# First MoE as x w2 w_out plus the positive part of two differences, its weights in memory by half tiles

## The chip, the cores and the metric

One core of one Trainium2 chip runs the whole program in one launch. The metric is the device time of one execution in microseconds. The kernel before took 809.39 us, the median of three runs from 806.94 to 810.66.

## What is computed

The reference has three stages on 4 x 768 = 3072 tokens of 384 values:

```python
for t in range(S):                                   # attention: B 4, H 8, S 768, D 48
    new_re = ar * S_re - ai * S_im                   # ar, ai: a_re, a_im, normalised
    new_im = ar * S_im + ai * S_re
    S_re, S_im = (new_re + kv, new_im)               # kv: outer product of k and v at t
    y[:, :, t] = np.einsum('bhd,bhde->bhe', q[:, :, t], S_re)

h = np.maximum(np.maximum(x @ w1, x @ w2), x @ w3)   # first MoE: 384 -> 768
x = h @ w_out                                        # 768 -> 384

for e in range(E):                                   # second MoE: 8 experts, one for each token
    mask = expert_idx == e
    h = np.maximum(x[mask] @ w1[e], 0.0)
    out[mask] = gate_w[mask, None] * (h @ w2[e])
```

The expert of a token is the largest of eight scaled cosines with `expert_emb`. Weights of the first MoE and `w_out` arrive as float64.

## The kernel before

**Two phases.** `phase1` does attention and the first MoE, `phase2` the second. Phase one takes the tokens in NU = 12 units of 256, three a batch. For unit u, `front(u)` normalises a, `mid(u)` builds prefix products of a on DVE (`sa`, `sb`, `Ct`, `X`), `back(u)` multiplies q and k by them and by their inverse (`m`, `rr`, `QK`) and DMAs the result into the matmul operand S (`S<-QK`). `attn(u, ch)` takes a tile of 128 tokens: products `pk`, `pa`, masked on DVE to `at`; `pT` and the running state; `py`; and y as x in two parts, `xhi` (ACT, rounded to f32r) and `xlo` (the rest, DVE or ACT). The 24 tiles are numbered 0 to 23, so `py20` is `py` of tile 20. `moe1(u)` is the first MoE. `route_early` sorts the first TE = 22 tiles' tokens to experts near the end of phase one. Phase two gathers the tokens by expert and runs the second MoE (lines 1268 to 1334).

**The first MoE, `moe1` (line 818).** Products of f32 precision are made of three f32r ones: hi by hi, hi by lo, lo by hi. For each of three groups `f2` of 256 of the 768 columns, and for each of w1, w2, w3 (m), two tiles of 128 columns take nine products of 256 tokens each, into PSUM tile `ph` (ring `h`, 3 buffers). ACT copies the first `ph` to `h`, DVE takes the maximum with the second and the third. For two of the groups (SPLIT = 2) ACT rounds `h` to `hhi` (1 buffer), DVE subtracts it into `hlo` (it shares the 2 buffers of `h`), and `px` gets three products of 392 columns for each f; the third group multiplies `h` itself in f32 by `wo`. The 392 columns are 384 of `w_out` and 8 of `w_out` times the normalised `expert_emb`, which give the routing logits.

**Weights, `weights` (line 709).** 24 tiles of 128 x 384 float64 words, six of `w_out` and eighteen halves of w1, w2, w3, are loaded as pairs of 32-bit words by POOL's DMA queue, and made into f32 from their bits: a sign (one of SIGNS = 4 tiles on DVE, the others by two ACT instructions), a scaled copy on ACT, two `scalar_tensor_tensor` on DVE. ACT then rounds the tile to its high part, and PE subtracts that from it in PSUM and ACT copies the rest:

```python
s.copy(hi, f)
t.matmul(pd, self.ident, f, start=True, stop=False)
t.matmul(pd, self.minus, hi, start=False, stop=True)
s.copy(rest, pd)
```

`ident` is f32 and `minus` the negated identity in f32r. The six tiles of `w_out` come first, then the others by m, i and half. There are 22 of these pairs, since the last two tiles of `w_out` stay f32. Raw tiles of w1 to w3 land in the memory of parts that are not yet written.

**Order.** `phase1` is not issued as written. `Recorder` (line 124) records each instruction with a key (KEYS: conv -0.9, attn -2.0, moe 0.3 and so on, plus the unit) and a bias for each kind and engine (BIAS, line 372), plans an order with modelled costs, and issues each engine's instructions in that order (line 368 in every row below). `keep_warm` (line 620, rows of L627) puts products that nobody reads into PE's gaps. Each engine works through its own order; SP's and POOL's are the DMA queues.

Of the kernel before, what the change touches and what calls it, by code (L numbers as in the profile page):

```python
# [9 lines left out]
F32 = mybir.dt.float32  # L10
# [11 lines left out]
W = 256  # L22
# [3 lines left out]
DM = H * D  # L26
# [97 lines left out]
class Recorder:  # L124
# [203 lines left out]
    def issue(self):  # L328
# [30 lines left out]
        for i in seq:  # L359
# [12 lines left out]
    BIAS = {"Gs": 1.84, "QKrg": -1.81, "Sg": 1.17, "Ss": 0.07, "Tss": 0.78, "Xv": 0.43, "arenv": 0.65, "cvhv": 0.53,  # L372
            "embss": -0.15, "fms": 2.46, "fmv": 3.34, "fyv": 0.76, "h_s": 0.7, "h_v": -0.65, "kt_s": -0.33, "pa_t": 1.07,
            "ph__t": -0.59, "pk_t": 1.3, "px__t": 0.15, "rrs": -0.38, "rrv": -0.75, "rwhig": -0.62, "rwlog": 1.88,
            "sav": -0.63, "slott": 2.08, "whi_s": 0.47, "wlo_s": 1.99, "xhis": 1.21, "xss": 0.26}
# [7 lines left out]
class Prog:  # L383
# [325 lines left out]
    def weights(self, split=True):  # L709
# [32 lines left out]
        ring, first = 0, 2 * self.SPLIT if split else 0  # L742
        for k, (src, m, i, c) in enumerate(todo):

            spot = None
            if split and m is not None:
                j = spots.index((m, i)) + (c > 0)
# [23 lines left out]
            whole = m is None and i >= first  # L771
            o = self.wo[:, i - first, :DM] if whole else f if split else self.w[:, m, i, c:c + n]
            v.scalar_tensor_tensor(o.bitcast(I32), raw[:, :, 0], 29, h, op0=ALU.logical_shift_right, op1=ALU.bitwise_or)
            if split and not whole:
                if m is not None and c == 0:
                    j = spots.index((m, i))
                    self.whi[m, i], self.wlo[m, i] = [self.tl(self.mw, [128, FF], f"w{x}{j}", 1, f"w{x}_{m}{i}", F32R)
                                                      for x in ("hi", "lo")]
                hi, rest = (self.wohi[:, i, :DM], self.wolo[:, i, :DM]) if m is None else \
                    (self.whi[m, i][:, c:c + n], self.wlo[m, i][:, c:c + n])  # L780
# [17 lines left out]
            if m is None and i == 5:  # L798
                if first:
                    s.copy(self.wohi[:, :, DM:], pG[:, :first])  # L800
                    v.tensor_sub(self.wolo[:, :, DM:], pG[:, :first], self.wohi[:, :, DM:].bitcast(F32))
                if first < 6:
                    v.tensor_copy(self.wo[:, :, DM:], pG[:, first:])
# [14 lines left out]
    def moe1(self, u):  # L818
# [5 lines left out]
        def mm(o, m, f):  # L824
            c = slice(f * 128, (f + 1) * 128)
            with q.group():
                for n, (w, x, i) in enumerate((w, x, i) for w, x in ((self.whi, xhi), (self.wlo, xhi), (self.whi, xlo))
                                              for i in range(3)):
                    t.matmul(o, w[m, i][:, c], x[:, i], start=n == 0, stop=n == 8)
        px = [self.tl(self.pf, [128, XC], "x1", 2, f"px1_{u}_{i}") for i in range(2)]  # L830
        for f2 in range(3):
            ps = []
            for m in range(3):
                ps.append(self.tl(self.pf, [128, 2, W], "h", 3, f"ph{u}_{f2}_{m}"))
                for f in range(2):
                    mm(ps[m][:, f], m, 2 * f2 + f)
# [5 lines left out]
            if f2 >= self.SPLIT:  # L842
                q.key = key
                for tt in range(2):
                    with q.group():
                        for f in range(2):
                            t.matmul(px[tt], h[:, f, tt * 128:tt * 128 + 128], self.wo[:, 2 * (f2 - self.SPLIT) + f],
                                     start=f2 + f == 0, stop=f2 + f == 3)
                continue
            hi = self.tl(pm, [128, 2, W], "hhi", 1, f"hhi{u}_{f2}", F32R)  # L850
            s.copy(hi, h)
            lo = self.tl(pm, [128, 2, W], "h", 2, f"hlo{u}_{f2}", F32R)
            v.tensor_sub(lo, h, hi.bitcast(F32))
# [196 lines left out]
    def phase1(self):  # L1050
        nc, tc = self.nc, self.tc
        with ExitStack() as ctx:
# [9 lines left out]
            self.wo = mw.tile([128, 6 - 2 * self.SPLIT, XC], F32, name="wo")  # L1062
            self.wohi = mw.tile([128, 2 * self.SPLIT, XC], F32R, name="wohi")
# [698 lines left out]
```

## Time and profile before

| | |
|---|---|
| Runs | 806.94, 809.39, 810.66 us |
| Profiled execution, its time | 811.25 us |
| Its span | 809.4 us, 19242 instructions |
| Mean granted clock of TensorE | 0.977 |
| PE, PEld | 750.9 us, 93%; 690.7 us, 85% |
| DVE, ACT, POOL | 78%, 55%, 12% |
| DMA | 107.46 MB, mean 133 GB/s |
| Weights converted, then the first `ph` | at 98.54 us |
| End of the last `px` of phase one, first product of the second MoE | 543.0 and 545.38 us |

The span is the time from the first to the last event of the profiled execution, whose own time is 1.9 us longer. A row of a group gives line, engine, operation, output<-inputs, shapes and count, then busy time, the mean length of one in ns, and idle time before them with what ended it. A row of a timeline gives its start and its busy time in us; xN stands for N like instructions in a row. Matmuls overlap, so what one costs is the distance between the starts of two. An f32 product is recorded as two matmuls. PE is the matrix engine, PEld its weight loads, PEclk the clock granted to it as a share of the full one, 1.2 of 2.4 GHz being 0.5.

### The profile page before, as it was taken

The page shows a single profiled execution, that of the slowest core. Times are in us where ns is not written, and L with a number is a line of the kernel's source. Part 1 is how long each engine was busy: PE and PEld are TensorE (multiplying, and loading weights), DVE is VectorE, ACT ScalarE, POOL GpSimd, SP SyncE. Part 2 cuts the span into 40 slices and gives each one's busy share as a digit, 9 for nine tenths or more (in the row PEclk, how much of TensorE's full clock was granted, in tenths as well). Part 3 has the DMA queues.
Part 4 walks back from the last instruction along what each step waited for, and adds up shares of the span by engine and source line. Part 5 has one row for each costly group of instructions (what it writes and reads, how often), then busy time and mean ns, then how long its engine had stood idle before and what let it go on. Part 6 is the DMA issues. An engine that isn't in the chain of part 4 may idle for free. (4 is left out here: it accounts for less than half of the span.)

```text
span 809.4 us, 19242 instructions
## 1 busy us (share of the span) xinstructions
PE 750.9 (93%) x7705; PEld 690.7 (85%) x7705; DVE 630.2 (78%) x1244; ACT 445.2 (55%) x1018; POOL 100.5 (12%) x156
## 2 busy tenths in 40 slices
PE   1757899999999999999999999999999999999996
PEld 0635789989898989999898989889989898989885
DVE  8999999999999999999988822659996455555420
ACT  8998746646647465665355341228545456554521
POOL 6301000000000000000000000021113312223111
PEclk9778999999999999999999999999999999999998
DMA  9706262571717345261624060051029694782500
GB/s 360 286 1 157 38 157 65 137 184 32 186 52 150 93 108 135 66 143 59 151 70 102 14 110 2 21 216 41 28 81 420 217 387 145 255 341 74 179 21 25
DMA packets 28754, 107.46 MB, mean 133 GB/s; under 512 B 5060, under 2 KB 8179, under 8 KB 25568
## 3 DMA queue, kind: packets, MB, share of 16 engines
q1 hardware_dynamic: 20432, 77.55, 32.2%
q0 software_dynamic: 7952, 28.21, 10.6%
q8 instruction: 62, 1.02, 0.5%
q10 hardware_dynamic: 272, 0.39, 0.2%
q14 instruction: 36, 0.29, 0.1%
HBM read 96.35 MB, written 10.62 MB: 132 GB/s over the span
## 5 line engine op out<-in xcount | busy, mean ns | idle before, releaser
L368 PE MATMUL ph<-xhi,whi 128*128 128x256 f32 x648 | 118.4, 291 | 0.4 <-DVE h L368 0.4
L368 PE MATMUL ph<-xlo,whi 128*128 128x256 f32 x648 | 113.0, 283 | 0.6 <-DVE xlo L368 0.6
L368 PE MATMUL ph<-xhi,wlo 128*128 128x256 f32 x648 | 112.7, 283 | 0.0
L368 PEld LDWEIGHTS ph<-xhi,whi 128*128 128x128 f32 x648 | 93.3, 191 | 6.9 <-issue 3.5
L368 PEld LDWEIGHTS ph<-xlo,whi 128*128 128x128 f32 x648 | 93.1, 192 | 1.0 <-DVE xlo L368 1.0
L368 PEld LDWEIGHTS ph<-xhi,wlo 128*128 128x128 f32 x648 | 93.0, 191 | 0.0
L1312 PE MATMUL ph<-xh,w1s 128*128 128x256 f32 x264 | 77.7, 294 | 0.0
L1274 DVE TENSOR_TENSOR w2l<-queue_q_buf,w2h 128x768 fp32r<-128x768 f32 x52 | 47.9, 955 | 37.3 <-ACT w2h L1273 37.3
L1312 PE MATMUL ph<-xh,w1l 128*128 128x256 f32 x264 | 75.4, 286 | 0.0
L1312 PE MATMUL ph<-xl,w1s 128*128 128x256 f32 x264 | 75.3, 285 | 0.0
L1328 PE MATMUL py<-w2h,hlo 128*128 128x384 f32 x200 | 67.1, 336 | 3.0 <-DVE hlo L1317 3.0
L1328 PE MATMUL py<-w2h,hhi 128*128 128x384 f32 x200 | 68.5, 343 | 0.0
L1328 PE MATMUL py<-w2l,hhi 128*128 128x384 f32 x200 | 67.1, 335 | 0.0
L368 DVE TENSOR_TENSOR h<-ph,h 128x512 f32<-128x512 f32 x72 | 49.5, 688 | 16.4 <-PE ph L368 15.0
L368 POOL DMA_DIRECT2D v<-v x24 | 13.0, 540 | 391.5 <-PE py L368 389.6
L1317 DVE SCALAR_TENSOR_TENSOR hlo<-ph,hhi 128x512 fp32r<-128x512 f32 x50 | 34.3, 687 | 32.7 <-ACT hhi L1316 32.6
L1316 ACT ACTIVATE hhi<-ph 128x512 fp32r<-128x512 f32 x50 | 29.9, 598 | 48.5 <-PE ph L1312 48.3
L1312 PEld LDWEIGHTS ph<-xh,w1s 128*128 128x128 f32 x264 | 51.2, 194 | 3.8 <-issue 3.1
L1312 PEld LDWEIGHTS ph<-xh,w1l 128*128 128x128 f32 x264 | 51.2, 194 | 0.5
L1312 PEld LDWEIGHTS ph<-xl,w1s 128*128 128x128 f32 x264 | 51.2, 194 | 0.0
L368 PE MATMUL pa<-S 112*128 112x128 f32 x384 | 49.1, 277 | 1.3 <-DVE at L368 0.7
L1273 ACT CAST w2h<-queue_q_buf 128x768 fp32r x52 | 40.7, 832 | 16.6 <-PE py L1328 15.5
(401 smaller groups left out, 1818.2 us busy)
## 6 DMA issues: line engine op xcount, KB each, us to landing
queue_q_buf<-w SPq DMA_DIRECT2D x26, 1536.0 KB
S<-QK SPq DMA_DIRECT2D x46, 289.1 KB
X<-a SPq DMA_DIRECT2D x11, 768.0 KB
QKr<-qk SPq DMA_DIRECT2D x11, 768.0 KB
w1m<-w SPq DMA_DIRECT2D x5, 1536.0 KB
w2m<-w SPq DMA_DIRECT2D x5, 1536.0 KB
v<-v POOLq DMA_DIRECT2D x24, 224.0 KB, 4.4
x1d<-x1s SPq DMA_DIRECT2D x22, 192.0 KB
```

The source lines that it names most:

```text
L368: getattr(getattr(self.nc, c[0]), c[1])(*c[2], **c[3])
L1273: s.copy(hi, b[:, c])
L1274: v.tensor_sub(lo, bv[:, c], hi.bitcast(F32))
L1312: t.matmul(ph[:, f], a, b, start=o == 0, stop=o == len(ops) - 1)
L1316: s.activation(hi, ph, AF.Relu).ins,
L1317: v.scalar_tensor_tensor(lo, ph, 0.0, hi.bitcast(F32), op0=ALU.max, op1=ALU.subtract).ins]
L1328: t.matmul(py, a[:, f, r], c[:, k % 4], start=o == 0, stop=o == 3 * KF - 1)
```

## The change

It rests on max(a, b, c) = b + max(0, a - b, c - b), so that the first MoE is x (w2 w_out) + max(0, x (w1 - w2), x (w3 - w2)) w_out.

- The host passes w2 a second time, transposed (`w2t`, six tiles of float64); tiles of w2 itself are no longer loaded. Tiles loaded are 24 again: six of `w2t` first (into the third buffer of ring `X`), then the first halves of w1 and w3, then the second halves, then `w_out`.
- For each half tile of w1 and w3 PE puts the f32 tile into PSUM and takes three transposed blocks of w2 off it by f32 products with `minus`; ACT rounds the difference to hi, PE subtracts that, ACT copies lo (`rest`). Both parts lie in the memory of the raw half tile.
- V = w2 w_out (384 x 392) is made by 18 f32 products (`pw0` to `pw2`, six each) and split into `vhi`, `vlo`.
- In `moe1`, V adds 18 f32r products of 392 columns to `px` at the start of a unit (at the end of it for unit 0). Two `ph` tiles for each group are left of three; ACT's copy becomes a Relu; one DVE maximum is left of two.
- `w_out` is split into `wohi`, `wolo` at the end, by four ACT copies and four DVE subtractions.
- BIAS, the table of biases, has other numbers. Lines after the table shift by up to 25.

```diff
@@ in the class Recorder
-    BIAS = {"Gs": 1.84, "QKrg": -1.81, "Sg": 1.17, "Ss": 0.07, "Tss": 0.78, "Xv": 0.43, "arenv": 0.65, "cvhv": 0.53,
...
+    BIAS = {"Cts": -0.91, "Cv": 0.78, "Gs": -0.3, "QKrv": -1.34, "QKs": -0.19, "Sg": 1.22, "Ss": 0.13, "Xg": 1.31,
...
@@ in weights
-        spots = [(m, i) for i in range(3) for m in range(3)]
-        todo = [(self.io["wo"][i], None, i, None) for i in range(6)]
-        todo += [(self.io["w123"][m, i, :, c:c + n], m, i, c) for m, i in spots for c in (0, n)]
+        out = [(self.io["wo"][i], None, i, None) for i in range(6)]
+        if split:
+            spots = [(m, i) for i in range(3) for m in (0, 2)]
+            todo = [(self.io["w2t"][f], 1, f, None) for f in range(6)]
+            w2t = self.tl(self.pp, [128, 3, L, 3 * NR], "X", 3, "w2t").rearrange("p c l b -> p (c l b)")
...
+        todo += [(self.io["w123"][m, i, :, c:c + n], m, i, c) for c in (0, n) for m, i in spots]
+        todo = todo + out
...
+        def rest(hi, lo, ps):
+            s.copy(hi, ps)
+            t.matmul(ps, self.minus, hi, start=False, stop=True, skip_group_check=True)
+            s.copy(lo, ps)
...
-                spot = f"w{'hi' if c else 'lo'}{j}" if j < len(spots) else None
-            if spot:
-                raw = self.tl(self.mw, [128, FF], spot, 1, "r" + spot, I32)
+            if split and c is not None:
+                raw = self.tl(self.mw, [128, FF], f"w{m}{i}{c}", 1, f"r{m}{i}{c}", I32)
...
-                    self.whi[m, i], self.wlo[m, i] = [self.tl(self.mw, [128, FF], f"w{x}{j}", 1, f"w{x}_{m}{i}", F32R)
...
-                s.copy(hi, f)
+                both = self.tl(self.mw, [128, 2, n], f"w{m}{i}{c}", 1, f"w_{m}{i}{c}", F32R)
+                self.whi[m, i, c // n], self.wlo[m, i, c // n] = both[:, 0], both[:, 1]
                 pd = self.tl(self.pf, [128, n], "h", 3, f"pd{k}")
                 with q.group():
-                    t.matmul(pd, self.ident, f, start=True, stop=False)
-                    t.matmul(pd, self.minus, hi, start=False, stop=True)
-                s.copy(rest, pd)
+                    t.matmul(pd, self.ident, f, start=True, stop=True)
+                    for b in range(3):
+                        t.matmul(pd[:, b * 128:(b + 1) * 128], w2t[:, c // 128 + b, i * 128:(i + 1) * 128],
+                                 self.minus.bitcast(F32), start=False, stop=True, skip_group_check=True)
+                rest(both[:, 0], both[:, 1], pd)
...
+        for f in range(2 * self.SPLIT):
+            s.copy(self.wohi[:, f], self.wo[:, f])
+            v.tensor_sub(self.wolo[:, f], self.wo[:, f], self.wohi[:, f].bitcast(F32))
+        for i in range(3):
+            pw = self.tl(self.pf, [128, XC], "h", 3, f"pw{i}")
+            with q.group():
+                for f in range(6):
+                    t.matmul(pw, w2t[:, f, i * 128:(i + 1) * 128], self.wo[:, f], start=f == 0, stop=f == 5)
+            rest(self.vhi[:, i], self.vlo[:, i], pw)
@@ in moe1
+        late = u == 0
+
+        def by_v():
+
+            for tt in range(2):
+                ts = slice(tt * 128, tt * 128 + 128)
+                with q.group():
+                    for n, (x, w, i) in enumerate((x, w, i) for x, w in ((xhi, self.vhi), (xhi, self.vlo), (xlo, self.vhi))
+                                                  for i in range(3)):
+                        t.matmul(px[tt], x[:, i, ts], w[:, i], start=n == 0 and not late, stop=n == 8 and late)
+        if not late:
+            by_v()
...
-            for m in range(3):
+            for m in (0, 2):
...
-            s.copy(h, ps[0])
+            s.activation(h, ps[0], AF.Relu)
             v.tensor_max(h, ps[1], h)
-            v.tensor_max(h, ps[2], h)
...
+        if late:
+            by_v()
@@ in the host's preparation of the inputs
+    w2t = f(i["moe_w2"][perm].T).reshape(6, 128, DM).view(np.int64)
```

The BIAS table and the new order of tiles move instructions on all engines. The places where the prediction speaks of that follow; numbers after names tell buffers apart.

DVE ahead of `xlo0`, the last operand of the first unit of the first MoE, before:

```order
L368 TENSOR_TENSOR sb_392<-Ct_144,X2_261 128x48
L368 TENSOR_TENSOR QKr1_260<-QKr1_260,rr1_329 128x768
L368 TENSOR_TENSOR Ct_144<-sb_392 128x24
L368 SCALAR_TENSOR_TENSOR xlo0_274<-py1_284,xhi0_273 128x3x128
L368 TENSOR_TENSOR sb_393<-Ct_144,X2_261 128x48
L368 SCALAR_TENSOR_TENSOR fm3_380<-fy3_381,X3_334 128x768
L368 TENSOR_TENSOR Ct_144<-sb_393 128x24
L368 SCALAR_TENSOR_TENSOR rr1_329<-rr1_329,QKr1_260 128x768
L368 TENSOR_TENSOR sb_394<-Ct_144,X2_261 128x48
L368 TENSOR_TENSOR QK1_330<-QKr1_260,X1_173 128x6x256
L368 TENSOR_TENSOR Ct_144<-sb_394 128x24
L368 TENSOR_TENSOR QK1_330<-rr1_329,X1_173 128x6x128
```

And now:

```order
L368 TENSOR_TENSOR rr1_311<-rr1_311 128x768
L368 TENSOR_TENSOR at1_1_268<-pa1_1_267,mask_66 128x512
L368 SCALAR_TENSOR_TENSOR rr1_311<-rr1_311,QKr1_245 128x768
L368 TENSOR_TENSOR X2_246<-sa_367 128x2x96
L368 SCALAR_TENSOR_TENSOR X2_246<-sa_367 128x96
L368 SCALAR_TENSOR_TENSOR fm3_359<-fy3_360,X3_316 128x768
L368 TENSOR_TENSOR sb_370<-X2_246 128x48
L368 TENSOR_TENSOR QK1_312<-rr1_311,X1_166 128x6x128
L368 TENSOR_TENSOR Ct_146<-sb_370 128x24
L368 TENSOR_TENSOR QK1_312<-rr1_311,X1_166 128x6x128
L368 TENSOR_TENSOR sb_371<-Ct_146,X2_246 128x48
L368 SCALAR_TENSOR_TENSOR xlo0_259<-py1_269,xhi0_258 128x3x128
```

The last `rr1` row, the three `QK1` rows (the widest of them, 128x6x256, ten rows above the piece) and the first `fm3` row stand ahead of `xlo0` now; they stood behind it.

PE in the attention of unit 0 (`pk0`, `pa0`, then `pT0`), before:

```order
L368 MATMUL pk0_1_265<-ident_61,S0_142 128x112 x4
L368 MATMUL pa0_1_269<-S0_142 128x128 x4
L368 MATMUL pd18_221<-cvh0_154,ident_61 128x384
L368 MATMUL pd18_221<-whi_02_219,minus_138 128x384
L368 MATMUL pk0_0_263<-ident_61,S0_142 128x112 x4
L368 MATMUL pd19_223<-cvh1_155,ident_61 128x384
L368 MATMUL pd19_223<-whi_02_219,minus_138 128x384
L368 MATMUL pa0_0_267<-S0_142 128x128 x4
L368 MATMUL pk1_0_276<-ident_61,S0_142 128x112 x4
L368 MATMUL pd20_227<-S1_143,ident_61 128x384
L368 MATMUL pd20_227<-whi_12_225,minus_138 128x384
```

And now:

```order
L368 MATMUL pk0_1_250<-ident_61,S0_144 128x112 x4
L368 MATMUL pG_204<-enT_164,wt22_214 128x8
L368 MATMUL pG_204<-enT_164,wt23_216 128x8 x3
L368 MATMUL pa0_1_254<-S0_144 128x128 x4
L368 MATMUL pw0_217<-wo_135,w2t_158 128x392 x6
L368 MATMUL pk0_0_248<-ident_61,S0_144 128x112 x4
L368 MATMUL pw1_218<-wo_135,w2t_158 128x392 x6
L368 MATMUL pa0_0_252<-S0_144 128x128 x4
L368 MATMUL pk1_0_261<-ident_61,S0_144 128x112 x4
L368 MATMUL pw2_219<-wo_135,w2t_158 128x392 x6
```

Where pairs `pd18` to `pd20` stood between the pieces of the attention, the three parts of the fold w2 w_out stand now.

DVE ahead of the `at` of tile 20 (`h9`: the first MoE of unit 9, `m11`: `back(11)`), before:

```order
L368 TENSOR_TENSOR h9_0_923<-ph9_0_1_921,h9_0_923 128x512
L368 TENSOR_TENSOR m11_0_1030<-X11_891,C11_1016 128x768
L368 TENSOR_TENSOR h9_0_923<-ph9_0_2_922,h9_0_923 128x512
L368 TENSOR_TENSOR m11_0_1030<-X11_891,C11_1016 128x768
L368 TENSOR_TENSOR hlo9_0_925<-h9_0_923,hhi9_0_924 128x512
L368 TENSOR_TENSOR X11_891<-m11_0_1030 128x2x384
L368 TENSOR_TENSOR m11_1_1031<-X11_891,C11_1016 128x768 x2
L368 TENSOR_TENSOR h9_1_929<-ph9_1_1_927,h9_1_929 128x512
L368 TENSOR_TENSOR X11_891<-m11_1_1031 128x2x384
L368 TENSOR_TENSOR h9_1_929<-ph9_1_2_928,h9_1_929 128x512
L368 TENSOR_TENSOR QK11_1029<-QKr11_963,X11_891 128x6x256
L368 TENSOR_TENSOR at20_0_970<-pa20_0_969,mask_66 128x512
```

And now:

```order
L368 TENSOR_TENSOR hlo9_0_882<-h9_0_880,hhi9_0_881 128x512
L368 TENSOR_TENSOR m11_0_982<-X11_849,C11_968 128x768 x2
L368 TENSOR_TENSOR X11_849<-m11_0_982 128x2x384
L368 TENSOR_TENSOR m11_1_983<-X11_849,C11_968 128x768 x2
L368 TENSOR_TENSOR X11_849<-m11_1_983 128x2x384
L368 TENSOR_TENSOR h9_1_885<-ph9_1_2_884,h9_1_885 128x512
L368 TENSOR_TENSOR QK11_981<-QKr11_918,X11_849 128x6x256
L368 TENSOR_TENSOR arena_1019<-mask_66,ident_61 128x128
L368 MEMSET arena_1019 128x176
L368 SCALAR_TENSOR_TENSOR rr11_980<-rr11_980 128x768
L368 MEMSET arena_1019 128x8
L368 TENSOR_TENSOR at20_0_925<-pa20_0_924,mask_66 128x512
```

Of the maxima of a group (`h9_1<-ph9_1_1`, `h9_1<-ph9_1_2`) one is left, and an `rr11` row stands ahead of `at20_0`.

## Rows read from the trace of the kernel before

**Rows 1.** The page, part 1: busy us (share of the span) xinstructions.

```profile
PE 750.9 (93%) x7705; PEld 690.7 (85%) x7705; DVE 630.2 (78%) x1244; ACT 445.2 (55%) x1018; POOL 100.5 (12%) x156
```

**Rows 2.** Stretches of the span; columns PE, PEld, DVE, ACT, POOL, PEclk, DMA, GB/s.

```profile
60.00:80.00 20.00, 14.85 (x71) 11.12 (x71) 19.97 (x51) 16.97 (x39) 2.74 (x5) 0.84 0.61 158
120.00:160.00 40.00, 39.31 (x516) 36.19 (x515) 38.76 (x75) 26.60 (x75) 1.10 (x2) 1.00 0.39 103
360.00:400.00 40.00, 40.00 (x445) 36.24 (x444) 38.59 (x86) 19.99 (x59) 1.07 (x2) 1.00 0.46 109
460.00:500.00 40.00, 40.00 (x427) 37.38 (x420) 12.56 (x18) 12.52 (x40) 1.07 (x2) 1.00 0.33 62
545.00:809.00 264.00, 251.23 (x1873) 236.32 (x1873) 153.66 (x264) 133.31 (x201) 60.53 (x56) 0.98 0.45 171
```

**Rows 3.** DVE's waits, 120 to 440 us: total, times, longest.

```profile
DVE fy L368 <- ACT fm L368: 3.0, 3, 1.8
```

**Rows 4.** PE's waits, 120 to 440 us.

```profile
PE pk L368 <- DMA S<-QK: 3.2, 4, 1.2
```

**Rows 5.** PE's timeline at the first `ph`: start, busy, instruction.

```profile
98.54 0.52 PE L368 MATMUL ph<-xhi,whi 128*128 128x256 f32 x3
```

**Rows 6.** PE's timeline: `pd` of the setup, `px` and `ph` of a unit.

```profile
71.16 0.81 PE L368 MATMUL pd<-S,ident 128*128 128x384 f32 x2
...
71.97 0.70 PE L627 MATMUL pk<-ident 128*128 128x112 f32 x5
...
79.92 1.64 PE L368 MATMUL pd<-cvh,ident 128*128 128x384 f32 x2 [1.69 <-ACT wlo L368]
...
81.68 0.63 PE L368 MATMUL pa<-S 112*128 112x128 f32 x2
...
472.68 0.34 PE L368 MATMUL px<-wolo,hhi 128*128 128x392 f32 x1
472.86 0.34 PE L368 MATMUL px<-wohi,hlo 128*128 128x392 f32 x1
...
479.00 0.52 PE L368 MATMUL ph<-xhi,wlo 128*128 128x256 f32 x3
479.36 0.52 PE L368 MATMUL ph<-xlo,whi 128*128 128x256 f32 x3
```

**Rows 7.** PE's timeline, `py20` and the last `px` of phase one.

```profile
459.46 1.05 PE L368 MATMUL py<-at,v 128*32 128x128 f32 x32
...
540.36 2.79 PE L368 MATMUL px<-wo,h 128*128 128x392 f32 x8
...
545.38 0.83 PE L1312 MATMUL ph<-xT,w1s 128*128 128x128 f32 x6
```

**Rows 8.** DVE's timeline at `xlo0` and between 445 and 464 us.

```profile
98.84 0.56 DVE L368 SCALAR_TENSOR_TENSOR xlo<-py,xhi 128x384 fp32r<-128x384 f32 x1
...
445.02 0.69 DVE L368 TENSOR_TENSOR h<-ph,h 128x512 f32<-128x512 f32 x1
445.62 0.95 DVE L368 TENSOR_TENSOR m<-X,C 128x768 f32<-128x768 f32 x1
446.49 0.68 DVE L368 TENSOR_TENSOR h<-ph,h 128x512 f32<-128x512 f32 x1
...
453.64 1.75 DVE L368 TENSOR_TENSOR QK<-QKr,X 128x1536 f32<-128x1536 f32 x1
455.31 1.28 DVE L368 TENSOR_TENSOR at<-pa,mask 128x512 f32<-128x512 f32 x2
...
462.19 1.83 DVE L368 TENSOR_TENSOR QK<-rr,X 128x768 f32<-128x768 f32 x2
```

**Rows 9.** Groups of DVE and ACT by line, 120 to 440 us.

```profile
L368 DVE TENSOR_TENSOR h<-ph,h 128x512 f32<-128x512 f32 x50 | 34.4, 687 | 1.3 <-PE ph L368 0.8
...
L368 ACT COPY h<-ph 128x512 f32<-128x512 f32 x25 | 14.6, 585 | 18.9 <-DVE hlo L368 15.3 <-PE ph L368 3.6
...
L368 ACT CAST hhi<-h 128x512 fp32r<-128x512 f32 x17 | 10.5, 619 | 20.9 <-PE px L368 12.1 <-DVE h L368 8.5
```

More of the change, by code (lines that the diff above doesn't have):

```diff
@@ L741, in weights @@
         v.tensor_copy(enT, ps)
-        ring, first = 0, 2 * self.SPLIT if split else 0
-        for k, (src, m, i, c) in enumerate(todo):
-            spot = None
-            if split and m is not None:
-                j = spots.index((m, i)) + (c > 0)
-                spot = f"w{'hi' if c else 'lo'}{j}" if j < len(spots) else None
-            if spot:
-                raw = self.tl(self.mw, [128, FF], spot, 1, "r" + spot, I32)
+        ring = 0
+        def rest(hi, lo, ps):
+            s.copy(hi, ps)
+            t.matmul(ps, self.minus, hi, start=False, stop=True, skip_group_check=True)
+            s.copy(lo, ps)
+        for k, (src, m, i, c) in enumerate(todo):
+            if split and c is not None:
+                raw = self.tl(self.mw, [128, FF], f"w{m}{i}{c}", 1, f"r{m}{i}{c}", I32)
             else:
@@ L798, in weights @@
             if m is None and i == 5:
[L799 to L803, printed above, removed]
+                v.tensor_copy(self.wo[:, :, DM:], pG)
+        if not split:
+            return
+        for f in range(2 * self.SPLIT):
[7 more added lines that the diff above has]
+            rest(self.vhi[:, i], self.vlo[:, i], pw)
     def sqrt_small(self, new, out, x, n):
@@ L824, in mm @@
         def mm(o, m, f):
-            c = slice(f * 128, (f + 1) * 128)
+            half, c = f // 3, slice(f % 3 * 128, f % 3 * 128 + 128)
             with q.group():
@@ L828, in mm @@
                                               for i in range(3)):
-                    t.matmul(o, w[m, i][:, c], x[:, i], start=n == 0, stop=n == 8)
+                    t.matmul(o, w[m, i, half][:, c], x[:, i], start=n == 0, stop=n == 8)
         px = [self.tl(self.pf, [128, XC], "x1", 2, f"px1_{u}_{i}") for i in range(2)]
+        late = u == 0
[8 more added lines that the diff above has]
+            by_v()
         for f2 in range(3):
             ps = []
-            for m in range(3):
+            for m in (0, 2):
                 ps.append(self.tl(self.pf, [128, 2, W], "h", 3, f"ph{u}_{f2}_{m}"))
                 for f in range(2):
-                    mm(ps[m][:, f], m, 2 * f2 + f)
+                    mm(ps[-1][:, f], m, 2 * f2 + f)
             h = self.tl(pm, [128, 2, W], "h", 2, f"h{u}_{f2}")
             key, q.key = q.key, u + self.KEYS["max"]
-            s.copy(h, ps[0])
+            s.activation(h, ps[0], AF.Relu)
             v.tensor_max(h, ps[1], h)
-            v.tensor_max(h, ps[2], h)
[L842 to L853, printed above, removed]
+            if f2 < self.SPLIT:
+                hi = self.tl(pm, [128, 2, W], "hhi", 1, f"hhi{u}_{f2}", F32R)
+                s.copy(hi, h)
+                lo = self.tl(pm, [128, 2, W], "h", 2, f"hlo{u}_{f2}", F32R)
+                v.tensor_sub(lo, h, hi.bitcast(F32))
             q.key = key
@@ L858, in moe1 @@
                         ts = slice(tt * 128, tt * 128 + 128)
-                        wh, wl = self.wohi[:, 2 * f2 + f], self.wolo[:, 2 * f2 + f]
-                        for k, (a, b) in enumerate(((hi, wh), (hi, wl), (lo, wh))):
-                            t.matmul(px[tt], a[:, f, ts], b, start=f2 + f + k == 0, stop=f2 + f + k == 5)
+                        if f2 < self.SPLIT:
+                            wh, wl = self.wohi[:, 2 * f2 + f], self.wolo[:, 2 * f2 + f]
+                            terms = (hi, wh), (hi, wl), (lo, wh)
+                        else:
+                            terms = (h, self.wo[:, 2 * f2 + f]),
+                        for k, (a, b) in enumerate(terms):
+                            t.matmul(px[tt], a[:, f, ts], b, start=late and f2 + f + k == 0,
+                                     stop=not late and f2 + f == 3 and k == len(terms) - 1)
+        if late:
+            by_v()
         for tt in range(2):
```

29 lines of the change are left out of this document (14 added, 15 removed).

## Prediction, made before the changed kernel was run

> **What bounds the kernel now.** I read the page's busy times first, then a table of stretches, then the waits of the two busy engines, then single rows. The page gives TensorE (PE) 93% of the span, its weight loads (PEld) 85%, VectorE (DVE) 78% and ScalarE (ACT) 55% [rows 1]; these are averages over three stages. The stretches tell them apart [rows 2]. From 120 to 400 us, where twelve units of 256 tokens go through attention and the first MoE, PE is busy 39.3 to 40.0 of 40 us and DVE 38.6 to 38.8. At 460 to 500 us DVE has only 12.6 of 40 to do and PE 40.0: the tail is PE's alone. From 545 us on the second MoE runs, 264 us with PE busy 251; the change does not enter it, so it only shifts. Before 100 us weights are converted, PE is busy 14.9 of 20 us at a granted clock of 0.84, and DVE is busy 19.97 of 20.
>
> Two engines can be busy while one waits for the other in small pieces. From 120 to 440 us DVE's longest sum of waits is 3.0 us, for an `fm` of ACT [rows 3], and PE's is 3.2 us, for a DMA [rows 4]. So in phase one neither waits to speak of, and both would have to become shorter for the kernel to gain; the change shortens both.
>
> At tile 20 (of 24) one sees which is later. DVE issues the last `at` at 455.31 and is through with it some 1.2 us later [rows 8]; PE takes it up at 459.46 [rows 7]. PE was late by about 3 us there, and from there to its last `px` it has 83.5 us of rows: eight records of 2.63 us (0.66 for each of four f32 products of 392 columns) from 540.36, so to 543.0 [rows 7].
>
> **What the change removes and adds on PE.** A unit has 3 x 6 x 9 = 162 f32r products of 256 columns for `ph`; three of them take 0.36 us (479.00 to 479.36 [rows 6]), one 0.12. Without w2 there are 108: −54 x 0.12 = −6.5 us. V adds 18 products of 392 columns at 0.18 (472.68 to 472.86 [rows 6]): +3.2 us. That is −3.24 a unit, −38.9 for twelve. The rest of PE's row (PE pays a few per cent above these pitches where it changes between f32 and f32r) I leave.
>
> **In the setup.** The fold w2 w_out is 18 f32 products of 392 columns, 18 x 0.66 = 11.9 us at full clock. Of the identity-and-`minus` pairs, 0.81 us each at full clock (71.16 to 71.97 [rows 6]), there were 22, 17.8 us; now twelve with three f32 subtractions of 128 columns, which I price as one more f32 product of 384 columns (0.81 less an f32r product of 0.18, 0.63): 12 x 1.44 = 17.3. So PE has some 11 us more before its first `ph`. PE had 5 idle us in 20 there [rows 2], so most of it lies beside DVE's work; what shows is that the fold stands in three pieces of 4 us in PE's order between the `pk` and `pa` of unit 0, and DVE's next `at` waits behind one. Bounds: nothing, if DVE has other rows ahead, and 5 us, a piece and its neighbours. I take 2.5. DVE itself converts 24 tiles in either kernel. Its order now has, ahead of `xlo0`, one `QK` row of 1536 elements, two of 768, an `rr` and an `fm` row that stood behind it: 1.67 (453.64 to 455.31) + 4 x 0.87 (445.62 to 446.49) [rows 8] = 5.2 us, of which 5.0 remain after small rows. That is work moved, not added, yet it delays `xlo0` (98.84 [rows 8]) and with it the first `ph` (98.54 [rows 5], which needs only the first half of x). First `ph`: 98.5 + 5.0 + 2.5 = 106.0.
>
> The changed sharing of memory moves SP's queue: X2's load waits for X0's place, so for the end of `back(0)`, and X3's for w2t's, so for the last piece of the fold; behind X2 in SP's queue stand the S writes of unit 0. I count 0 to 3 us for this, inside the 5 above, since the engines have other units to work on. The split of each half tile into its own memory and the copies of wo at the end cost four ACT and four DVE rows of 392 elements; a row of 384 as `xlo0` takes 0.47 (98.84 to the next row), so 1.9 on DVE; ACT is far from full.
>
> **On DVE.** One maximum of 512 elements goes in each of 36 groups. Its row lasts 0.69 us, yet the next starts 0.60 after it (445.02 to 445.62 [rows 8]), so 0.60 is what it gives back: 21.6 us in all. Ahead of the `at` of tile 20 there are 29 of them, counted in the two orders, 17.4; with 1.9 added and 0.87 for an `rr` now ahead of it, −14.7.
>
> **The sum by the two paths.** By PE: 106.0 + (543.0 − 98.5) − 38.9 = 511.6, against 543.0: −31. By DVE: `at` of tile 20 done at 456.6 − 14.7 + 2.5 = 444.4; behind it PE had 83.5 us of rows, of which, counted in the two orders, 126 `ph` products go (−15.1) and 24 px products of 0.18 come (+4.3), so 72.7: 517.1, −26. By PE alone it would reach that `at` at about 439, so DVE becomes the later one by some 5 us. Part of what delayed DVE up to there was PE, and that part shrinks, so I take −28, with −26 and −31 as its ends and 3 us more on either side for the DMA and the start.
>
> The Trainium skill says otherwise on one point: "Perfetto Trace Analysis", "Identifying the Most-Contended Engine", holds the busy share of matmuls for a bad measure, wants that of weight loads, and names the engine of highest occupancy as the one to shorten. By it DVE (97% from 120 to 400 us against some 90% for PEld [rows 2]) sets the pace and the answer would be the −26 of the DVE path. The trace does not bear out that PE has a tenth to spare: PE's own waits there are as small as DVE's [rows 3, 4].
>
> The profiled execution took 811.25 us, 1.9 above the median of the runs, 809.39. −28 on it is 783.2, on the median 781.4; I say 782.
>
> **Rivals.**
> A (the forecast): both engines stay dense and the end moves by 26 to 31 us. 60%. Own range 777 to 787.
>
> B: the fold runs at the lower clock. The pair of 0.81 us took 1.76 at 79.92 (to 81.68 [rows 6]), 2.17 times as long, and the granted clock was 0.84 between 60 and 80 us [rows 2]. Then the fold takes 25.8 us in place of 11.9, DVE waits up to 14 us more at unit 0, and the two paths give −12 and −17: 794 by their middle. For it: PE idled a quarter of that stretch. Against it: PE gets more to do there, and dummy products fill its gaps. 22%.
>
> C: the start is not delayed at all, DVE follows PE, and the whole −38.9 arrives: 770.5. For it: DVE's rows ahead of `xlo0` were only moved; against it: DVE's path would then be 12 us too late. 8%.
>
> D: slower. In a group of two f tiles the path copy of `ph`, maximum, `hhi`, `hlo`, `px` is serial: 0.59 + 0.69 + 0.62 + 0.69 [rows 9] and four hand-overs, about 3.4 us when nothing else queues on ACT and DVE, and `h` has two buffers, `hhi` one. PE covered it with the 54 `ph` products of the next group, 6.5 us; now with 36, 4.3. ACT already waited 15.3 us for `h` buffers that `hlo` held, and 20.9 ahead of `hhi` [rows 9], but PE paid nothing. If the shorter cover exposes more than 28/36 = 0.8 us in each group, the gain is gone; at 1.0 us the kernel is slower by 8 us, 817. For it: only 0.9 us of cover is left, while DVE's queue is in order and full. Against it: V's products (3.2 us a unit) and attention's rows can stand between, and the longest sum of PE's waits up to 440 us is for a DMA [rows 4]. At a part of that price the gain shrinks towards nothing. 5% slower, 5% within 0.5%.
>
> **How the numbers follow.** 0.5%, about 4 us, is what a measurement of this kernel can tell from no change. Faster by more: A, B and C, 0.90; the same 0.05; slower 0.05. The range goes from C's 770 to just beyond B's middle, 798; outside are D, the rest of B and what would beat C.
>
> **What would show it.** Right: first `ph` near 106 us; `px1_11` ending near 515; 108 `ph` products in a unit and DVE still over 93% busy from 120 to 400 us, with PE at 96% or more; the second MoE as long as before, 264 us. Fold pieces at 4 us mean full clock, at 8 us B. Wrong: PE waiting for `hlo` or `h` by more than 0.5 us in a group (D), a first `ph` after 115 us (B), or one before 100 with the whole of phase one shorter by 38 us (C). If DVE falls well below 90% while PE stays full, DVE was not the later path, and the gain is PE's alone.

## The result, and the profile after

The changed kernel takes 778.01 us (median of four runs, 776.86 to 778.26) against 810.02 us of the kernel before on the same chip (four runs, 806.94 to 811.65): a ratio of 0.9606, 95% interval 0.9575 to 0.9638. That is 32 us less. The forecast was 782, with 770 to 798 as its range. The profiled execution has a span of 775.9 us, 33.5 less than before.

Part 1 of the page, against [rows 1]:

```profile
PE 719.6 (93%) x7318; PEld 657.1 (85%) x7318; DVE 607.1 (78%) x1211; ACT 441.5 (57%) x1007; POOL 104.6 (13%) x156
```

DVE works 23 us less, 36 x 0.60 = 21.6 of it the maxima, and PE 31 us less. Their shares of the span are those of before, 93% and 78%. The stretches, against [rows 2]:

```profile
60.00:80.00 20.00, 16.87 (x96) 15.34 (x96) 17.38 (x50) 15.01 (x33) 3.83 (x7) 0.76 0.80 189
120.00:160.00 40.00, 37.81 (x486) 34.44 (x485) 39.41 (x76) 24.26 (x68) 1.07 (x2) 1.00 0.44 110
360.00:400.00 40.00, 39.74 (x538) 37.26 (x537) 38.64 (x73) 20.73 (x49) 1.61 (x3) 1.00 0.36 82
440.00:480.00 40.00, 40.00 (x479) 36.02 (x475) 9.50 (x14) 15.25 (x48) 1.07 (x2) 1.00 0.32 63
```

PE and DVE are both nearly full from 120 to 400 us, as they were (only PE's first 40 us have 37.8 in place of 39.3), and the tail is still PE's alone. The setup has a granted clock of 0.76 between 60 and 80 us where it was 0.84. The two engines' waits from 120 to 440 us, against [rows 3, 4], VectorE's first:

```profile
DVE G L368 <- ACT G L368: 1.2, 1, 1.2
DVE at L368 <- PE pa L368: 1.1, 3, 0.5
```

```profile
PE pk L368 <- DMA S<-QK: 2.1, 2, 1.6
PE pa L368 <- DVE at L368: 0.9, 4, 0.3
```

Single rows of PE's timeline, for [rows 5, 7], show where the time went:

```profile
107.17 0.97 PE L368 MATMUL ph<-xhi,w 128*128 128x256 f32 x6 [0.92 <-ACT xhi L368]
...
439.89 1.06 PE L368 MATMUL py<-at,v 128*32 128x128 f32 x32
...
509.44 2.79 PE L368 MATMUL px<-wo,h 128*128 128x392 f32 x8
512.08 0.49 PE L368 MATMUL pxg<-ident,xg 128*128 128x128 f32 x3
...
514.18 1.06 PE L1336 MATMUL ph<-xT,w1s 128*128 128x128 f32 x8
```

| Stretch | Before | After | Difference | Forecast by PE's path |
|---|---|---|---|---|
| Start to the first `ph` | 98.5 | 107.2 | +8.6 | +7.5 |
| First `ph` to `py20<-at` | 360.9 | 332.7 | -28.2 | -28 (106.0 to about 439) |
| `py20<-at` to the end of the last `px` | 83.5 | 72.2 | -11.3 | -10.8 |
| To the first product of the second MoE | 2.4 | 2.1 | -0.3 | 0 |
| Second MoE to the end | 264.0 | 261.7 | -2.3 | 0 |

The last column adds up to PE's path, -31; the prediction itself took -28, between that and DVE's path, -26. The last row is no work of the change: that stretch was between 261.4 and 264.7 us in the nine profiles of this study whose tokens went to the same experts, and both ends belong to variants of the kernel before.

### The profile page after: what moved, and what is told of

Same layout as the page of the kernel before. It is cut to its first block, busy times and chain, and to the rows that moved or that the text cites. A ratio compares the mean times of both kernels' runs of the same rounds, so it can differ in the third digit from the quotient of the medians.

```text
span 775.9 us, 18425 instructions
## 1 busy us (share of the span) xinstructions
PE 719.6 (93%) x7318; PEld 657.1 (85%) x7318; DVE 607.1 (78%) x1211; ACT 441.5 (57%) x1007; POOL 104.6 (13%) x156
## 3 DMA queue, kind: packets, MB, share of 16 engines
q1 hardware_dynamic: 20432, 77.55, 33.5%
q0 software_dynamic: 7952, 28.21, 11.3%
## 5 line engine op out<-in xcount | busy, mean ns | idle before, releaser
L368 PE MATMUL ph<-xhi,w 128*128 128x256 f32 x864 | 134.0, 291 | 0.9 <-ACT xhi L368 0.9
L368 PEld LDWEIGHTS ph<-xhi,w 128*128 128x128 f32 x864 | 114.3, 191 | 8.3 <-issue 4.7
L368 PE MATMUL ph<-xlo,w 128*128 128x256 f32 x432 | 75.3, 283 | 0.4 <-DVE xlo L368 0.4
L368 PEld LDWEIGHTS ph<-xlo,w 128*128 128x128 f32 x432 | 62.0, 191 | 0.6 <-DVE xlo L368 0.6
L368 PE MATMUL pa<-S 112*128 112x128 f32 x384 | 51.7, 279 | 2.2 <-DVE at L368 1.7
L368 PEld LDWEIGHTS pa<-S 112*128 112x128 f32 x384 | 48.2, 193 | 4.5 <-DVE at L368 2.9
L368 DVE TENSOR_TENSOR sa<-X 128x384 f32<-128x384 f32 x84 | 46.5, 554 | 0.7
L1292 DVE TENSOR_TENSOR w1l<-queue_q_buf,w1s 128x1536 fp32r<-128x1536 f32 x22 | 38.6, 1759 | 9.3 <-PE ph L1336 7.4
```

Source lines behind the costliest of these rows:

```text
L368: getattr(getattr(self.nc, c[0]), c[1])(*c[2], **c[3])
L1292: v.tensor_sub(wl[k], av.rearrange("p (a b) -> p a b", b=FF2)[:, :, c], w1[k].bitcast(F32))
```

## The experiments

In five of the six experiments that left something of phase one out, the tokens went to other experts and the second MoE took some 240 us longer. For those only the start of the second MoE counts: 545.38 us before, 514.18 after. (The sixth, PE's saving alone in the kernel before, kept the experts, and its whole time counts too.) Each variant has one trace. The first `ph` came at 97.3 to 100.6 us in the three traces that share the kernel before's setup and order, and at 106.8 to 109.0 in the five that share the changed kernel's, so a difference of 1 to 3 us between two traces is not clear of chance by itself. Most experiments keep the planned order: the planner sees the whole program, and what is left out or done twice is decided only when the instructions are issued. `issued` names what is issued in place of an operation:

```diff
-            for c in o.calls:
+            for c in self.issued.get(id(o), o.calls):
```

**Each saving alone.** The first question was whether PE or DVE paces phase one, before and after. In the kernel before, without the first maximum of a group:

```diff
             v.tensor_max(h, ps[1], h)
+            q.issued[id(q.ops[-1])] = []
             v.tensor_max(h, ps[2], h)
```

> The kernel before in its own order without the first of the two maxima of a group (36 DVE rows, 21.6 us), so x w2 is left out of the maximum though its products are still made: the change's saving on DVE alone. Theory P (PE was the later one, by 3 us at tile 20): no more than 0 to 3 us gained, 807 to 809. Theory D: 15 to 17 us gained, 793.

The second MoE starts at 544.57 us in place of 545.38. DVE's saving alone gives 0.8 us; as the first `ph` came 2.0 us later in this trace (100.55), though nothing ahead of it was changed, it is 2.8 from there on. Either is little beside 17.4. The stretch from 120 to 440 us in the kernel before, then in this one:

```profile
120.00:440.00 320.00, 315.68 (x4053) 292.41 (x4052) 306.03 (x582) 183.71 (x488) 9.68 (x18) 1.00 0.45 109
```

```profile
120.00:440.00 320.00, 317.54 (x4070) 294.54 (x4069) 295.56 (x563) 184.47 (x491) 9.68 (x18) 1.00 0.45 110
```

DVE's busy time falls by 10.5 us there, PE's rises by 2. Much of DVE's freed time became waits for PE. Between 98.8 and 456.6 us they were 1.0 us for `h` and 0.9 for `at` in the kernel before, and now are:

```profile
DVE h L368 <- PE ph L368: 5.3, 9, 0.9
DVE at L368 <- PE pa L368: 5.0, 10, 1.0
```

And its `at` of tile 20 starts 1.0 us sooner than at [rows 8], or 3.0 counted from `xlo0`, though 29 maxima ahead of it are gone:

```profile
100.86 0.55 DVE L368 SCALAR_TENSOR_TENSOR xlo<-py,xhi 128x384 fp32r<-128x384 f32 x1
...
454.32 1.43 DVE L368 TENSOR_TENSOR at<-pa,mask 128x512 f32<-128x512 f32 x2
```

So with less to do DVE waited for PE: the later path of the kernel before was PE's.

The other half, PE's saving alone, in the kernel before with 27 of a unit's 54 products by w2 left out:

```diff
                     t.matmul(o, w[m, i][:, c], x[:, i], start=n == 0, stop=n == 8)
+            if m == 1:
+                x = q.ops[-1].calls[:4 + f % 2]
+                q.issued[id(q.ops[-1])] = x[:-1] + [(*x[-1][:3], {**x[-1][3], "stop": True})]
```

> The kernel before in its own order with half of the products by w2 left out (27 of 54 a unit, 4 or 5 of each nine), so that PE alone gets the change's saving, 3.24 us a unit, 38.9 in all, and DVE keeps both maxima; h is then not the reference's, and only the trace up to the second MoE counts. If DVE follows PE by no more than the 3 us seen at tile 20, those 3 us and 63 products behind that tile (7.6 us) are gained: the second MoE starts near 535 in place of 545.4. If PE alone paces, 507 to 510.

The start is at 535.30, 10.1 us sooner of 38.9, and the one run took 801.78 us against 811.71. The first theory had the sum, 535, but not its parts: tile 20 comes 6.4 us sooner than at [rows 7], not 3 (1.2 of them stood already at the first `ph`, at 97.33), and what lies behind it is shorter by 3.7, not by 7.6. That the two errors cancel is luck.

```profile
453.07 1.06 PE L368 MATMUL py<-at,v 128*32 128x128 f32 x32
```

DVE is now the fuller engine, and PE waits for the S writes and for DVE's `h`:

```profile
120.00:440.00 320.00, 302.40 (x3860) 272.56 (x3861) 307.19 (x597) 182.99 (x489) 9.68 (x18) 0.99 0.46 110
```

```profile
PE pk L368 <- DMA S<-QK: 6.9, 5, 2.3
PE ph L368 <- DVE h L368: 5.5, 11, 0.8
```

The same from the other side, the changed kernel with each maximum done twice:

```diff
             v.tensor_max(h, ps[1], h)
+            q.issued[id(q.ops[-1])] = q.ops[-1].calls * 2
```

> The changed kernel in its own order, each of the 36 maxima done twice, so that DVE has back the 36 x 0.60 = 21.6 us that the change took from it, while PE keeps its saving. Theory P (PE paces phase one, and DVE was only 3 us ahead of it at tile 20: 436.9 against 439.9): the 17.4 us that fall ahead of that tile use up the 3 us and delay the rest, so 778 + 14 = 792. Theory D (DVE paces it already): all 17.4 us, 795 to 796. A third, that DVE has slack in plenty: 778 to 782.

798.37 us against 808.12, a ratio of 0.984 (0.977 to 0.992). In the trace, which is of the slowest of the four runs, the second MoE starts at 536.78, 22.6 us later than in the changed kernel and about where PE's saving alone put it; 1.8 us of that stood already at the first `ph` (108.98). That is more than theory P's 14 and nearer to D's 17 to 18, but the interval of the ratio, 6 us to either side, holds both. DVE is as full as before, and PE loses busy time:

```profile
120.00:440.00 320.00, 302.95 (x3827) 275.88 (x3826) 310.88 (x592) 183.98 (x487) 9.65 (x18) 0.99 0.44 107
```

PE's busy time in that stretch falls by 13.5 us (316.45 in the changed kernel): it waits 5.7 us for `h` ahead of `px`, 4.2 for `at` and 4.0 for the S writes.

**The changed kernel, with less still.** Without V's products:

```diff
                         t.matmul(px[tt], x[:, i, ts], w[:, i], start=n == 0 and not late, stop=n == 8 and late)
+                q.issued[id(q.ops[-1])] = []
...
-                            t.matmul(px[tt], a[:, f, ts], b, start=late and f2 + f + k == 0,
-                                     stop=not late and f2 + f == 3 and k == len(terms) - 1)
+                            t.matmul(px[tt], a[:, f, ts], b, start=f2 + f + k == 0,
+                                     stop=f2 + f == 3 and k == len(terms) - 1)
```

> The changed kernel in its own order without the 18 products of a unit by V, so x w2 w_out is left out of the first MoE: PE has 38.9 us less. Theory P with DVE 3 us ahead: the 3 us and the products behind tile 20 (some 2.5 units, 8 us), so 778 - 11 = 767. Theory D: the 8 us alone, 770. PE alone without any tie to DVE: 778 - 39 = 739.

```profile
442.91 1.05 PE L368 MATMUL py<-at,v 128*32 128x128 f32 x32
...
512.38 7.87 PE L1337 MATMUL ph<-xT,w1s 128*128 128x128 f32 x69
```

Only 1.8 us sooner, though PE has 38.9 us less to do. None of the three numbers was right; the nearest is that of DVE as the pace. The 1.8 are two parts: tile 20 comes 3.0 us later than in the changed kernel (442.91 against 439.89, where the first `ph` differ by 0.1), and what lies behind it is 4.8 shorter, about the 4.3 us of the 24 products of V there; the 8 us expected there were a miscount. Up to tile 20 PE's work turned into waits and into a lower clock, and DVE stayed nearly as full as it was:

```profile
120.00:440.00 320.00, 292.33 (x3762) 264.00 (x3761) 307.18 (x600) 189.75 (x507) 9.65 (x18) 0.98 0.46 111
```

```profile
PE pa L368 <- DVE at L368: 11.8, 6, 3.7
PE pa L368 <- ACT kt L368: 4.5, 2, 3.0
```

The granted clock is 0.98 from 120 to 440 us; single stretches of 40 us had 0.96.

Without the last maximum (the same edit as in the kernel before, at the one maximum that is left):

> The changed kernel in its own order without its last maximum (h is the Relu of the first difference alone), so DVE has 21.6 us less still. Theory P: 0 to 3 us gained, 775 to 778. Theory D: 15 to 17 us gained, 762.

The start is at 510.15, 4.0 us sooner of 21.6: near theory P. Now DVE has spare time and PE is full:

```profile
120.00:440.00 320.00, 318.34 (x4090) 294.49 (x4090) 299.27 (x576) 192.72 (x513) 10.19 (x19) 1.00 0.46 111
```

Both at once:

> The changed kernel in its own order without V's products and without the last maximum, both at once (x w2 w_out and the second difference are left out). Apart they moved the start of the second MoE from 514.2 to 512.4 and 510.2. If DVE and PE pace phase one together, each covering for the other, both at once give far more than the sum of 5.8: DVE's 17.4 us ahead of tile 20 and 4 us of products behind it, so a start near 490 to 495. If a third thing (ACT, the S writes, the two buffers of h) paces it, 506 to 510.

The start is at 502.17, 12.0 us sooner, which lies between the two answers: twice the sum of the two alone, 5.8, and half of what both paths would allow. Neither engine is full any more, and PE's waits are for `at`, for the S writes and for ACT's `kt`:

```profile
120.00:440.00 320.00, 298.60 (x3940) 272.31 (x3939) 298.52 (x578) 192.10 (x515) 10.19 (x19) 0.98 0.47 114
```

```profile
PE pa L368 <- DVE at L368: 10.4, 5, 3.6
PE pk L368 <- DMA S<-QK: 3.7, 2, 3.0
PE pa L368 <- ACT kt L368: 2.5, 2, 1.9
```

| Start of the second MoE, us | PE's work as it is | less by 38.9 |
|---|---|---|
| Kernel before | 545.4 | 535.3 |
| Kernel before, DVE less by 21.6 | 544.6 | 514.2 (the change) |
| Changed kernel | 514.2 | 512.4 |
| Changed kernel, DVE less by 21.6 | 510.2 | 502.2 |

In the first two rows the change is not only the two savings: it has a new order, and its first `ph` came 8.6 us later. Counted from the first `ph`, PE's saving alone gave 8.9 us, DVE's alone 2.8, and the change 39.8, no less than the 38.9 that PE was spared. The last two rows are of one order throughout.

**The setup.** The fold left out, but for one of its six terms:

```diff
                     t.matmul(pw, w2t[:, f, i * 128:(i + 1) * 128], self.wo[:, f], start=f == 0, stop=f == 5)
+            last = q.ops[-1].calls[-1]
+            q.issued[id(q.ops[-1])] = [(*last[:3], {**last[3], "start": True})]
             rest(self.vhi[:, i], self.vlo[:, i], pw)
```

> The changed kernel in its own order with 15 of the 18 products of the fold left out (V is then made of one of its six terms), so that PE has 9.9 us less ahead of the first ph at full clock. The output changes the routing, so only the trace up to the second MoE counts. If DVE's own rows (5 us moved ahead, 1.9 us of wolo) make the later first ph, it comes at 105 to 106 us in place of 107.2 and the second MoE starts 1 to 2 us sooner, 512 to 513. If the fold makes it, 99 to 101 us, and 506 to 509.

```profile
105.77 0.98 PE L368 MATMUL ph<-xhi,w 128*128 128x256 f32 x6 [0.62 <-ACT xhi L368]
```

The first `ph` is 1.4 us sooner and the second MoE starts at 513.41, 0.8 sooner, so the fold is not what makes the first `ph` late. The 1.4 are not its price at an equal clock, either: without it PE idled, and the granted clock was 0.59 and 0.56 in the two stretches from 92 to 100 us where the changed kernel has 1.00. What sets the first `ph` in the changed kernel is a row of DVE, by way of ACT:

```profile
104.91 0.95 DVE L368 SCALAR_TENSOR_TENSOR fm<-fy,X 128x768 f32<-128x768 f32 x1
```

```profile
105.89 0.84 ACT L368 ACTIVATE fy<-fm 128x768 f32<-128x768 f32 x1 [0.80 <-DVE fm L368]
106.64 0.47 ACT L368 ACTIVATE xhi<-py 128x384 fp32r<-128x384 f32 x1
```

The first `ph` waits for `xhi` (the row at 107.17 above), `xhi` stands behind `fy` in ACT's order, and `fy` waits for `fm`, one of the rows moved ahead. In the run without the fold the same three rows stand 1.4 us sooner. Another wait, 2.1 us for `pG`, stays in it; it is there since the tiles of w_out come last (with them earlier, in the next run, that row has no wait):

```profile
79.84 0.21 DVE L368 COPY wo<-pG 128x48 f32<-128x48 f32 x1 [2.06 <-PE pG L368]
```

The tiles of w_out earlier, right behind w2t:

```diff
-        todo += [(self.io["w123"][m, i, :, c:c + n], m, i, c) for c in (0, n) for m, i in spots]
         todo = todo + out
+        todo += [(self.io["w123"][m, i, :, c:c + n], m, i, c) for c in (0, n) for m, i in spots]
```

> The changed kernel with the six tiles of w_out loaded and converted right after those of w2t, ahead of the differences, so that the fold can run before the attention of unit 0; the planner orders anew. If the fold between the pieces of that attention is what delays the first ph, it comes some 3 to 5 us sooner (103) and the time is 773 to 775. If DVE's own rows set the first ph, it stays at 106 to 108 us and the time at 776 to 780. A fold at the lower clock that holds up the differences would give a first ph after 110 us and 781 or more.

782.52 us against 813.0, ratio 0.963 (0.960 to 0.967); the first `ph` is at 106.42, 0.8 us sooner. But the planner did not put the fold ahead of the attention of unit 0. It stands in one piece behind it, just ahead of the first `ph`:

```profile
93.05 12.02 PE L368 MATMUL pw<-wo,w2t 128*128 128x392 f32 x36
```

The next row of PE starts at 104.60, and PE has no idle time from there to the first `ph`, so here PE sets it (`xlo0` is there at 105.44); what an earlier fold would give stays untested. The rest of the order lost more, for the second MoE starts at 518.28, 4.1 later. As a whole the variant is not clear of the changed kernel's 0.9606.

**Memory, order, and POOL.** The kernel before with the raw half tiles in the memory of their own parts, and nothing else changed:

```diff
+                raw = self.tl(self.mw, [128, FF], f"w{m}{i}{c}", 1, f"r{m}{i}{c}", I32)
...
+                    both = self.tl(self.mw, [128, 2, n], f"w{m}{i}{c}", 1, f"w_{m}{i}{c}", F32R)
+                    self.whi[m, i, c // n], self.wlo[m, i, c // n] = both[:, 0], both[:, 1]
```

> The kernel before with one part of the change, the memory: each raw half tile lies in the memory of its own high and low parts, for all eighteen half tiles, and nothing else is changed; the planner orders anew. If the memory moves no bound, 806 to 812 with the first ph at 97 to 100 us. If raw tiles had waited for memory, the first ph comes sooner and the time falls by as much, 800 to 805.

816.75 us against 813.0, ratio 1.005 (1.002 to 1.007), the first `ph` at 104.53: later by 6 us, which neither answer had. The memory, with an order planned anew, gains nothing. I put the loss down to the new order, which the planner wrote with biases made for the old memory; that was not tried apart.

The changed kernel with the old table of biases:

```diff
-    BIAS = {"Cts": -0.91, "Cv": 0.78, ...
+    BIAS = {"Gs": 1.84, "QKrg": -1.81, ...
```

> The changed kernel with the table of biases of the kernel before, so the planner writes another order for the same work. If the gain is the work that went from PE and DVE, the order costs little: 776 to 784, with the first ph between 104 and 110 us. If the new table is what makes the gain, most of it goes: 790 to 805.

786.82 us against 813.0, ratio 0.968 (0.963 to 0.972), between the two answers: the work makes most of the gain, and the new table some 0.7 points of 3.9, though the intervals still touch. The first `ph` is at 111.51, 4.3 us later than with the new one.

The four subtractions for wolo on POOL, the order planned anew, and then with the order kept:

```diff
-            v.tensor_sub(self.wolo[:, f], self.wo[:, f], self.wohi[:, f].bitcast(F32))
+            q.gpsimd.tensor_sub(self.wolo[:, f], self.wo[:, f], self.wohi[:, f].bitcast(F32))
```

> The changed kernel with the four subtractions that make wolo on POOL in place of DVE, 1.9 us of DVE work less; the planner orders anew. If DVE's rows pace phase one up to tile 20, 776 (1 to 2 us gained, at the edge of what can be measured); if PE paces it, no change, 778. If the later wolo holds up px of unit 0, 779 to 781.

785.59 us against 813.0, ratio 0.968 (0.964 to 0.973), slower than all three answers.

```diff
             v.tensor_sub(self.wolo[:, f], self.wo[:, f], self.wohi[:, f].bitcast(F32))
+            q.issued[id(q.ops[-1])] = [("gpsimd", *q.ops[-1].calls[0][1:])]
```

> The changed kernel in its own order with the four wolo subtractions issued on POOL in place of DVE at the same place. It takes 1.9 us of DVE's setup away without a new order. If DVE sets the first ph and the pace, 776 to 777 and the first ph near 105.5; if a new order was what cost the run with wolo on POOL its 6 us, this one is no slower than 778; if POOL's rows slow DVE down or come too late for the first px, 780 or more.

780.86 us against 811.71, ratio 0.964 (0.960 to 0.967): no gain, and not clear of the changed kernel. The first `ph` stays at 106.96, since these rows stand behind `xlo0`. The other half of a per cent of the run before would be its new order, though the two intervals overlap. POOL took 1.4 us for each, where on DVE the second stands 0.57 behind the first (the rows are POOL's in this kernel and DVE's in the changed one):

```profile
105.85 5.70 POOL L368 TENSOR_TENSOR wolo<-wo,wohi 128x392 fp32r<-128x392 f32 x4
```

```profile
112.84 0.56 DVE L368 TENSOR_TENSOR wolo<-wo,wohi 128x392 fp32r<-128x392 f32 x1
...
113.41 0.56 DVE L368 TENSOR_TENSOR wolo<-wo,wohi 128x392 fp32r<-128x392 f32 x1
```

No variant that computes the same was faster than the change as it is.

## Why the prediction was right

**What bounds the kernel** was right in the main, and the experiments make it sharper. "Both would have to become shorter for the kernel to gain": PE's saving alone gave 10.1 us of 38.9 (3.7 of them behind tile 20), DVE's alone 0.8, and the change 31.2. The sum of the parts would have forecast 11. In one order, from the changed kernel on, the two savings gave 1.8 and 4.0 alone and 12.0 together.

**PE's sum** was right to 0.5 us at its end: 511.6 forecast, 512.1 measured (the row at 509.44, then 512.08). The count of products (-3.24 us a unit) and the tail (72.7 us forecast, 72.2 measured) hold.

**The start** was forecast at 106.0 and came at 107.2. Its two terms were 5.0 us of DVE rows moved ahead of `xlo0` and 2.5 us of waits for the fold. `xlo0` came 9.1 us later than at [rows 8]:

```profile
79.45 0.21 DVE L368 COPY wo<-pG 128x48 f32<-128x48 f32 x1 [2.05 <-PE pG L368]
...
107.94 0.55 DVE L368 SCALAR_TENSOR_TENSOR xlo<-py,xhi 128x384 fp32r<-128x384 f32 x1
...
435.38 0.69 DVE L368 TENSOR_TENSOR at<-pa,mask 128x512 f32<-128x512 f32 x1 [0.55 <-PE pa L368]
...
436.27 0.69 DVE L368 TENSOR_TENSOR at<-pa,mask 128x512 f32<-128x512 f32 x1
```

The wait of 2.1 us for `pG` was not in the sum. Without the fold the first `ph` came 1.4 us sooner, and of DVE's two waits for `pa` from 80 to 108 us only the second, 0.7 us, stands behind a piece of it, so the fold's own part is nearer to 1 than to 2.5, as far as one trace tells. Nor did the moved rows act as the prediction had it, by `xlo0`: the first `ph` followed `fm`, and the two `QK` rows of 768, which stand behind `fm`, delayed `xlo0` alone. Those waits, and the pieces of the fold:

```profile
DVE at L368 <- PE pa L368: 1.2, 2, 0.7
```

```profile
81.11 5.48 PE L368 MATMUL pw<-wo,w2t 128*128 128x392 f32 x12
86.43 0.55 PE L368 MATMUL pk<-ident,S 112*128 112x112 f32 x4
86.81 4.13 PE L368 MATMUL pw<-wo,w2t 128*128 128x392 f32 x12
90.78 1.06 PE L368 MATMUL pa<-S 112*128 112x128 f32 x8
```

The first took 5.3 us (81.11 to 86.43), partly at the lower clock (granted 0.52 from 80 to 84 us, 1.00 from 84 to 100), the second 4.0 (86.81 to 90.78), as forecast for full clock. Rival B, the fold at the lower clock, did not come: the clock rose within the first piece. The wolo rows, which the prediction lists with the setup, stand behind it, at 112.84 and later.

**The step that failed is "DVE becomes the later one by some 5 us", from which -26 was made one end and -28 the middle.** The `at` of tile 20 was forecast done at 444.4 and was done some 0.6 us behind its row at 436.27. I had taken the 357.8 us between `xlo0` and that point in the kernel before (98.8 to 456.6) and taken 29 maxima off it. Now the same stretch takes 329.0 us, 28.8 less, where the rows removed or moved ahead make 17.4 + 5.2, less 1.9 for wolo and 0.9 for an `rr`: 19.8. The prediction's ground for going beyond -26, "part of what delayed DVE up to there was PE, and that part shrinks", does not account for the other 9 us. Here is the stretch in the kernel before, with DVE's waits for PE in it, and in the changed kernel:

```profile
98.84:456.60 357.76, 353.05 (x4356) 328.59 (x4356) 342.83 (x660) 199.44 (x527) 9.68 (x18) 1.00 0.44 107
```

```profile
DVE h L368 <- PE ph L368: 1.0, 4, 0.3
DVE at L368 <- PE pa L368: 0.9, 2, 0.5
```

```profile
107.94:436.90 328.96, 325.00 (x4025) 299.41 (x4024) 318.70 (x630) 200.28 (x535) 9.65 (x18) 1.00 0.47 115
```

DVE's busy time fell by 24.1 us, its idle time by 4.7 (14.9 to 10.3), and of that the waits put down to PE by 0.6 (1.0 + 0.9 for `h` and `at` to 0.2 + 1.1). So about half of the 9 us is busy time, most of it because the rows that stayed stand closer together in the new order. The other half is idle time, most of which the profile puts down to no engine. The old distance less the rows removed does not hold in a new order. And DVE was not the later one: PE took up tile 20 about 3 us behind DVE in both kernels (456.6 and 459.46, 436.9 and 439.89). PE's path, -31, was the end to take.

**The Trainium skill's rule** ("Perfetto Trace Analysis", "Identifying the Most-Contended Engine"), by which DVE would set the pace of the kernel before, would have been wrong here: the run without a maximum gained 0.8 us of 21.6, and the one with less for PE 10.1 of 38.9. In the changed kernel it fits better, with 4.0 of DVE's 21.6 and 1.8 of PE's 38.9.

**The rivals.** C, the whole -38.9, fell with the start, which was 8.6 us later. D, the chain behind `ph` laid open by fewer products, did not show: PE waited nowhere for `hlo`, and for `at` 0.9 us in 320. With the maxima doubled PE did lose 13.5 us of busy time in that stretch, 5.7 of them in waits for `h`; whether that is the chain of one group or DVE's pace as a whole is not shown. Two side sums are off by about one, without effect: B's middle of -12 and -17 is 795, not 794, and in C DVE's path is 13 us too late, not 12.

**What stays open** is what in the new order shortened DVE's stretch by those 9 us; how far the gap between the 28 us forecast and the 32 measured is that step (some 3 us by the path) and how far the second MoE's own scatter of 3 us; and which of the waits left with both engines' work reduced (`at`, the S writes, `kt`) would have to go first.

## What to carry to other kernels

When two engines are both full and neither waits, price a change on each path to a common row, and take what is off a path only as far as the other path allows: here a saving on one alone gave 4% to 26% of itself, and on both more than the sum of the two. Busy shares of 96% and 99% do not tell which one paces; leaving a row of one out at issue, with the order kept, and looking at the common row does. Look at the first common row as well, since traces of one setup differ by 2 to 3 us there. And where a planner writes the order anew, compare with a frozen order first: variants that were ordered anew lay 0.3% to 0.8% behind, and the one edit that was tried both ways 0.3% with its order kept and 0.8% without.

## What the runs showed that I had not expected

216 products of 392 columns, 38.9 us of PE's work, cost 1.8 us: V's part of the first MoE is nearly free. Behind tile 20 it costs its price, 4.8 us; up to there leaving it out made PE wait for DVE, with a granted clock of 0.96 in four of the eight stretches of 40 us, and tile 20 came 3.0 us later. Doubling the maxima cost some 20 us in the runs' times and 20.8 in the trace from the first `ph` on, about their own 21.6, although ACT and POOL were far from full.
